# Upper halves of two weight matrices, laid out in 16 blocks whose starts differ by 512 bytes

## The chip, the core and the metric

The kernel runs on one core of one Trainium2 chip. Such a core has five engines that run side by side and wait for each other through semaphores: TensorE (PE, the matmuls; its loads of the stationary operand are shown apart as PEld), VectorE (DVE), ScalarE (ACT), GpSimd (POOL) and SyncE (SP), which starts the DMAs. Operands lie in SBUF, 128 partitions of bytes; matmuls write to PSUM. The metric is the time of one execution on the device in microseconds, the median of several runs.

## The reference

A sliding-window attention (64 keys back, 8 heads of 64) feeds a two-layer block with a softmax-weighted activation and a norm. Cut to what matters:

```python
scores = scale * q @ k^T                    # 8 batches, 8 heads, 576 positions, 64 wide
attn   = softmax(where(0 <= i - j < 64, scores, -1e9))
x      = (attn @ v)                         # 4608 rows x 512
h      = x @ w_in                           # 4608 x 1024
solu   = h * softmax(h)
ln     = (solu - mean) / sqrt(var + 1e-6) * g_ln
out    = ln @ w_out                         # 4608 x 512
```

## The kernel before

The 4608 rows are worked in 36 tiles of 128. For each tile the kernel loads q, k and v, computes the scores on TensorE (line 460), the softmax on DVE, ACT and POOL (lines 475 to 500), transposes it, multiplies by v (line 559), then runs the two matrix products of the block: `moe_in` (line 603, x times w_in into `pH`) and `moe_out` (line 737, the normed rows times w_out into `pO`).

Those two products are made of three matmuls in place of one, to keep float32 accuracy with one pass per matmul: each operand is split into an upper half (rounded to the type that TensorE reads in one pass, float32r) and a lower half (what the rounding left out). A product is then x upper times w upper, x upper times w lower, x lower times w upper. So the names are: `xH`, `xL` and `yH`, `yL` for the rows, `w_inH` and `w_outH` for the upper halves of the weights, and the ring tile `w` for the lower halves (`WL`). In each matmul the rows are the stationary operand (128 x 128, loaded by a LDWEIGHTS of its own) and 512 columns of a weight are the moving operand. A row tile takes 24 matmuls of line 603 and 24 of line 737; in each, 16 move an upper half and 8 a lower half, in the order H, lower, H, lower, H, H. Tiles 0 to 2 (line 590) and 0 to 1 (line 724) use plain float32 matmuls on unsplit weights instead.

The upper halves are written once, by `split` (lines 386 to 400): for each of 16 blocks of 512 columns ACT writes the block through `WH(i, x)` and DVE reads it back to make the lower half. From then on only TensorE reads them. Before the change a block is a slice of `w_inH` [128, 4, 1024] or of `w_outH` [128, 8, 512]. Each block is 2048 bytes of a partition.

Where they lie follows from the order of the declarations. The tiles ahead of them and the unnamed tile `shift` put `w_inH` at byte 20416 of a partition, which leaves 448 when divided by 512. Both weights are 16384 bytes, so each of the 16 blocks begins at remainder 448. `g_sb` (32 bytes), the unnamed tile `gap` (960) and `neghalf` (32 with its rounding up) fill 1024, and all the rings behind (`qk`, `w`, `xH`, `yH`, ...) have sizes that are multiples of 512, so each row operand, each of its 512-byte column groups, and each lower half begins at remainder 448 too. A LDWEIGHTS reads 512 bytes of a partition.

The order of the work is made by the class `Plan`, a list scheduler with fixed costs that looks at operations and tiles, not at addresses. All engines then run their instructions in the planned order.

Of the kernel before, what the change touches and what calls it, by code (L numbers as in the profile page):

```python
# [9 lines left out]
F32 = mybir.dt.float32  # L10
F32R = mybir.dt.float32r
# [8 lines left out]
P = 128  # L20
# [47 lines left out]
SPL = 3  # L68
RATE = 240

PADS = 12
PAD_S = 0
PAD_P = 0
# [153 lines left out]
def tile_window_attention_solu_moe(  # L227
# [19 lines left out]
    NT, DM = out.shape  # L247
    w_in, w_out = w_in.bitcast(I32), w_out.bitcast(I32)
    DFF = w_in.shape[1] // 2
# [3 lines left out]
    NC = DM // P  # L253
    NF = DFF // P
# [4 lines left out]
    const = ctx.enter_context(tc.tile_pool(name="const", bufs=1))  # L259
# [25 lines left out]
            nc.gpsimd.memset(t[first * WIN:(first + 1) * WIN, :WIN], NEG)  # L285

    const.tile([P, 272], F32, name="shift")
    w_inH = const.tile([P, NC, DFF], F32R, name="w_inH")
    w_outH = const.tile([P, NF, DM], F32R, name="w_outH")
    g_sb = const.tile([P, NF], F32, name="g_sb")  # L290
    const.tile([P, 240], F32, name="gap")
    neghalf = const.tile([P, 1], F32, name="neghalf")
    nc.gpsimd.memset(neghalf, -0.5)

# [20 lines left out]
        return T("w", NW + i, [P, 2, 512], F32R)  # L315

    def WH(i, x):
        if i < NC:
            return w_inH[:, i, x * 512:(x + 1) * 512]
        return w_outH[:, 2 * (i - NC) + x]  # L320

    def weight_block(i, src):

# [62 lines left out]
    def split(i):  # L386

        for x in range(2):
            reads = [("w", i), ("w", i, x), ("w", NC + 1 if i < NC else NW - 1)]
            last = reads[:2] + [("H", i, x)], [("w", NW + i, x)]  # L390
            if i < NC:
                plan.op("ACT", 600, lambda x=x: nc.scalar.copy(WH(i, x), W32(i)[:, x]), reads, [("H", i, x)])
                plan.op("DVE", 690, lambda x=x: nc.vector.tensor_sub(
                    WL(i)[:, x], W32(i)[:, x], WH(i, x).bitcast(F32)), *last, port=True)
                continue
            f = 2 * (i - NC) + x
            plan.op("ACT", 600, lambda x=x, f=f: nc.scalar.mul(WH(i, x), W32(i)[:, x], g_sb[:, f:f + 1]),
                    reads + [("g",)], [("H", i, x)])
            plan.op("DVE", 690, lambda x=x, f=f: nc.vector.scalar_tensor_tensor(
                WL(i)[:, x], W32(i)[:, x], g_sb[:, f:f + 1], WH(i, x).bitcast(F32), ALU.mult, ALU.subtract), *last, port=True)  # L400
# [27 lines left out]
    def SS(t):  # L428
        return T("sS", t, [P, H, P])
# [38 lines left out]
    def softmax(t):  # L468
# [16 lines left out]
        def rec():  # L485
            return T("rec", t, [P, H], pool=st)
# [3 lines left out]
        for o in range(0, H, n):  # L490
# [6 lines left out]
            for h in range(o, o + n):  # L497
                plan.op(engine, cost, lambda h=h: v.tensor_scalar(  # L498
                    SS(t)[:, h], SS(t)[:, h], rec()[:, h:h + 1], 0.0, ALU.mult, ALU.add),
                    [R], [("sS", t, h)], PAD_S if t >= PADS else 0, port=True)  # L500

# [3 lines left out]
    def XP(t):  # L505
        return T("raw", NW + 2 * t, [P, 4, 2, 512], U16)

    def cross(t):
        if t < CROSS_P:
            return  # L510
        for x in range(2):
# [4 lines left out]
                XP(t)[:, 2 + x].rearrange("p w (h n) -> p (w h) n", h=4), XP(t)[:, x].rearrange("p w n -> p (w n)")),  # L516
                [("raw", NW + 2 * t, x)], [("raw", NW + 2 * t, 2 + x)], PAD_P if t >= PADS else 0, t > SPL)

# [137 lines left out]
    def EP(t, h):  # L656
        return XB(t)[:, h]

    def TP(t, h):
        return XB(t)[:, 2 + h].rearrange("p w (f n) -> p w f n", f=4)  # L660

    def moe_cross(t):
        if not crosses(t):
            return
        for h in range(2):
# [4 lines left out]
                TP(t, h).rearrange("p w f n -> p (w f) n"), EP(t, h).rearrange("p w n -> p (w n)")),  # L670
                [("raw", NW + 2 * t + 1, h)], [("raw", NW + 2 * t + 1, 2 + h)], PAD_E if t >= PADS else 0, t > SPL)

# [227 lines left out]
```

## Time and profile before

| | |
|---|---|
| runs | 511.93, 512.82, 513.01 us; median 512.82 |
| span of the profiled execution, first to last instruction | 510.9 us |
| around the span (median less span) | 1.9 us |
| busy: PE, PEld, DVE, ACT, POOL | 492.1, 392.4, 409.8, 355.6, 314.5 us |
| matmuls of lines 603 and 737 | 1608, of which 1072 move an upper half |

The profiled execution has no time of its own beside its span; the 1.9 us is the median of the runs less that span. A matmul's duration in the rows includes its way through the array, so two matmuls that follow each other overlap; what a matmul costs is the distance from its start to the next one's start. I call that its spacing. The chain of waits, in order of time, sums up such runs: a piece "5.44 PE pH L603 x24" is 24 spacings.

### The profile page before, as it was taken

What the parts mean: (1) busy time and instruction counts of PE and PEld (TensorE: products, weight loads), DVE (VectorE), ACT (ScalarE), POOL (GpSimd) and SP (SyncE); (2) the same over time, 40 slices, a digit from 0 to 9 for tenths busy, and PEclk for the clock granted to TensorE, in tenths of its full rate; (3) what the DMA queues carried; (4) which work ended last, traced back from release to release, by engine and by line L of the source; (5) the groups of instructions that cost most, each with busy time, mean ns of one, the idle gap of its engine ahead of it and who ended that gap; (6) DMA issues with size and microseconds to landing.
All of it is one profiled execution on the core that took longest, in us unless ns stands there. A gap on an engine that the chain in (4) does not pass through costs nothing.

```text
span 510.9 us, 11601 instructions
## 1 busy us (share of the span) xinstructions
PE 492.1 (96%) x4064; PEld 392.4 (77%) x4064; DVE 409.8 (80%) x1176; ACT 355.6 (70%) x960; POOL 314.5 (62%) x566
## 2 busy tenths in 40 slices
PE   2889999999999999999999999999999999999996
PEld 1445577888788888888888888888888888888885
DVE  5998997888796989787978898887878878977531
ACT  4589795868686777777776868686859586865331
POOL 4388467664757475758574858584848485936430
PEclk9999999999999999999999999999999999999999
DMA  8994446966889989898889797879897969764301
GB/s 321 412 410 177 116 120 119 234 156 147 173 219 148 234 164 229 171 223 163 229 151 243 143 250 145 250 141 247 132 244 144 267 117 222 124 131 103 83 21 43
DMA packets 150762, 94.09 MB, mean 184 GB/s; under 512 B 135088, under 2 KB 135344, under 8 KB 150320
## 3 DMA queue, kind: packets, MB, share of 16 engines
q1 hardware_dynamic: 150704, 93.35, 76.7%
q8 instruction: 32, 0.52, 0.5%
q14 instruction: 26, 0.21, 0.1%
HBM read 50.86 MB, written 9.44 MB: 118 GB/s over the span
## 4 chain that ended last, share of the span: by engine, by line
PE 85%; DVE 4%; ACT 2%; POOL 2%; DMA 2%; issue 0%; SPq 0%; ACTq 0%; DVEq 0%; POOLq 0%
PE pH L603 34%; PE pO L737 34%; PE pO L559 6%; PE pS L460 6%; PE pO L724 3%; PE pH L590 1%; DMA raw<-raw 1%; ACT sS L480 1%; POOL sS L498 1%; PE pS L700 1%; DVE e L623 1%; DVE mst L618 1%; DMA y<-ot 1%; ACT e L620 0%; DVE w L368 0%
## 5 line engine op out<-in xcount | busy, mean ns | idle before, releaser
L498 POOL TENSOR_SCALAR sS<-sS,rec 128x128 f32<-128x128 f32 x280 | 149.2, 554 | 10.8 <-PE pS L460 7.4
L480 ACT ACTIVATE sS<-sS,nmx 128x128 f32<-128x128 f32 x288 | 111.5, 389 | 1.5 <-DVE nmx L475 1.4
L737 PE MATMUL pO<-w_outH,yH 128*128 128x512 f32 x272 | 108.2, 398 | 0.0
L737 PE MATMUL pO<-w,yH 128*128 128x512 f32 x272 | 106.1, 390 | 0.0
L603 PE MATMUL pH<-w_inH,xH 128*128 128x512 f32 x264 | 103.7, 393 | 0.8 <-DVE mst L623 0.8
L603 PE MATMUL pH<-w,xH 128*128 128x512 f32 x264 | 101.8, 389 | 0.0
L737 PE MATMUL pO<-w_outH,yL 128*128 128x512 f32 x272 | 83.9, 389 | 0.0
L512 ACT COPY raw<-sS 128x1024 uint16<-128x1024 uint16 x64 | 66.6, 1046 | 22.9 <-POOL sS L498 22.7
L603 PE MATMUL pH<-w_inH,xL 128*128 128x512 f32 x264 | 81.9, 389 | 0.0
L640 POOL TENSOR_SCALAR e<-e,mst 128x512 f32<-128x512 f32 x72 | 66.8, 936 | 3.9
L632 POOL TENSOR_SCALAR mst<-mst 128x1 f32<-128x1 f32 x36 | 19.9, 553 | 79.8 <-ACT sq L629 42.9
L522 DVE COPY PT<-raw 128x1024 uint16<-128x1024 uint16 x64 | 50.0, 789 | 19.9 <-DMA raw<-raw 19.7
L573 ACT CAST xH<-pO 128x512 fp32r<-128x512 f32 x33 | 19.3, 586 | 63.5 <-PE pO L559 63.4
L737 PEld LDWEIGHTS pO<-w_outH,yH 128*128 128x128 f32 x272 | 51.0, 188 | 12.7 <-issue 2.6
L618 DVE TENSOR_REDUCE mst<-pH 128x1 f32<-128x1024 f32 x36 | 44.0, 1221 | 20.1 <-PE pH L603 20.0
L737 PEld LDWEIGHTS pO<-w_outH,yL 128*128 128x128 f32 x272 | 51.1, 188 | 10.9
L603 PEld LDWEIGHTS pH<-w_inH,xH 128*128 128x128 f32 x264 | 49.6, 188 | 12.2 <-PE pO L737 1.2
L737 PEld LDWEIGHTS pO<-w,yH 128*128 128x128 f32 x272 | 51.1, 188 | 10.0
L603 PEld LDWEIGHTS pH<-w_inH,xL 128*128 128x128 f32 x264 | 49.6, 188 | 10.6 <-issue 0.2
L603 PEld LDWEIGHTS pH<-w,xH 128*128 128x128 f32 x264 | 49.6, 188 | 10.4 <-issue 0.2
L626 POOL TENSOR_SCALAR mst<-mst 128x1 f32<-128x1 f32 x36 | 18.9, 524 | 62.3 <-DVE mst L623 56.5
L629 ACT ACTIVATE sq<-e,mst 128x1024 bf16<-128x1024 f32 x36 | 41.4, 1150 | 21.6 <-POOL mst L626 21.6
(71 smaller groups left out, 852.3 us busy)
## 6 DMA issues: line engine op xcount, KB each, us to landing
qk<-qk SPq DMA_DIRECT2D x36, 640.0 KB, 5.9
v<-vS SPq DMA_DIRECT2D x36, 512.0 KB, 4.7
y<-ot SPq DMA_DIRECT2D x35, 256.0 KB, 2.7
raw<-w_out SPq DMA_DIRECT2D x4, 1024.0 KB, 12.0
raw<-w_in SPq DMA_DIRECT2D x3, 1024.0 KB, 11.5
raw<-raw SPq DMA_TRANSPOSE x126, 3.2
raw<-w_in SPq DMA_DIRECT2D x2, 512.0 KB, 6.2
y<-ot SPq DMA_DIRECT2D x2, 128.0 KB, 1.7
```

The lines of the kernel that those rows point to most:

```text
L460: nc.tensor.matmul(PS(t, p // 2)[half * WIN:(half + 1) * WIN, r, p], q[rs, p, half * WIN:(half + 1) * WIN], keys, start=True, stop=True)
L480: plan.op("ACT", 390, lambda h=h: nc.scalar.activation(SS(t)[:, h], SS(t)[:, h], AF.Exp, bias=cols("nmx", h), scale=-1.0, accum_out=cols(" ...
L498: plan.op(engine, cost, lambda h=h: v.tensor_scalar(SS(t)[:, h], SS(t)[:, h], rec()[:, h:h + 1], 0.0, ALU.mult, ALU.add), [R], [("sS", t, ...
L512: plan.op("ACT", 1050, lambda x=x: nc.scalar.copy(XP(t)[:, x], SS(t)[:, 4 * x:4 * x + 4].bitcast(U16).rearrange("p h (n w) -> p w (h n)", ...
L522: plan.op("DVE", 740, lambda x=x: nc.vector.tensor_copy(PT(t)[:, 4 * x:4 * x + 4].bitcast(U16).rearrange("p h (n w) -> p h w n", w=2), XP( ...
L559: nc.tensor.matmul(PX(t, p)[r * D:(r + 1) * D, p, ks], V(t, half)[:, h * D:(h + 1) * D], PT(t)[:, h, ks], start=True, stop=True)
L603: plan.op("PE", 235, lambda n=n, c=c, d=d, x=x, w=w: nc.tensor.matmul(PH(t)[:, d * 512:(d + 1) * 512], x(t)[:, c], WH(c, d) if w is WH els ...
L618: plan.op("DVE", 1225, lambda: nc.vector.tensor_reduce(nmax(), PH(t), axis=AX.X, op=ALU.max, negate=True), [("pH", t)], [key(0)])
L629: plan.op("ACT", 1150, lambda: nc.scalar.activation(T("sq", t, [P, DFF], BF16), E(t), AF.Square, bias=nmean(), scale=1.0, accum_out=ss()), ...
L632: plan.op("POOL", 240, lambda: nc.gpsimd.tensor_scalar(kk(), ss(), se(), se(), ALU.mult, ALU.mult), [key(1), key(3)], [key(5)])
L640: plan.op("POOL", 770, lambda h=h, hs=hs: nc.gpsimd.tensor_scalar(E(t)[:, hs], E(t)[:, hs], nmean(), kk(), ALU.add, ALU.mult), [key(4), ke ...
L737: plan.op("PE", 235, lambda n=n, f=f, i=i, x=x, y=y, w=w: nc.tensor.matmul(PO(), y(t)[:, f], w(i, x), start=(n == 0), stop=(n == len(passe ...
```

## The change

The two tiles become flat, with 64 columns (256 bytes) more each. Block n begins STEPS[n] bytes behind its old place within its tile. Blocks don't overlap, since the steps rise within each tile. `w_inH` stays at byte 20416; `w_outH` moves up by the 256 bytes that `w_inH` has grown by; `gap` shrinks by the 512 that both have grown by, so all that lies behind it stays where it was.

```diff
+STEPS = [16, 32, 48, 64, 96, 112, 128, 192, 0, 80, 144, 160, 176, 208, 224, 240]
...
     const.tile([P, 272], F32, name="shift")
-    w_inH = const.tile([P, NC, DFF], F32R, name="w_inH")
-    w_outH = const.tile([P, NF, DM], F32R, name="w_outH")
+    WOFF = [512 * n + x // 4 for n, x in enumerate(STEPS)]
+    w_inH = const.tile([P, 8 * 512 + 64], F32R, name="w_inH")
+    w_outH = const.tile([P, 8 * 512 + 64], F32R, name="w_outH")
     g_sb = const.tile([P, NF], F32, name="g_sb")
-    const.tile([P, 240], F32, name="gap")
+    const.tile([P, 112], F32, name="gap")
...
     def WH(i, x):
-        if i < NC:
-            return w_inH[:, i, x * 512:(x + 1) * 512]
-        return w_outH[:, 2 * (i - NC) + x]
+        w, n = (w_inH, 2 * i + x) if i < NC else (w_outH, 8 + 2 * (i - NC) + x)
+        o = WOFF[n] - n // 8 * 4096
+        return w[:, o:o + 512]
```

Counted from the remainder 448 that everything else keeps, the eight blocks of `w_inH` now begin 16, 32, 48, 64, 96, 112, 128 and 192 bytes on. The eight of `w_outH` begin 256, 336, 400, 416, 432, 464, 480 and 496 bytes on, the 256 of the moved tile included. No block keeps the remainder 448. The order of instructions is the same on all five engines, and so are their shapes and the tiles that they wait for.

## Rows read from the trace of the kernel before

**Rows 1.** The page's busy times and the chain that ended last.

```profile
PE 492.1 (96%) x4064; PEld 392.4 (77%) x4064; DVE 409.8 (80%) x1176; ACT 355.6 (70%) x960; POOL 314.5 (62%) x566
...
PE 85%; DVE 4%; ACT 2%; POOL 2%; DMA 2%; issue 0%; SPq 0%; ACTq 0%; DVEq 0%; POOLq 0%
```

**Rows 2.** Busy us by engine in stretches, then granted clock, DMA share, GB/s.

```profile
100.00:200.00 100.00, 99.23 (x902) 82.11 (x901) 83.05 (x242) 71.33 (x188) 62.29 (x114) 1.00 0.87 188
200.00:300.00 100.00, 100.00 (x881) 83.50 (x880) 83.93 (x230) 72.69 (x197) 66.88 (x117) 1.00 0.85 194
300.00:400.00 100.00, 100.00 (x795) 83.15 (x795) 83.45 (x253) 73.74 (x204) 67.46 (x120) 1.00 0.89 187
400.00:460.00 60.00, 60.00 (x550) 50.18 (x547) 51.09 (x157) 44.65 (x123) 39.09 (x66) 1.00 0.80 168
```

**Rows 3.** The chain in order of time: start us, length us, engine, tile, line.

```profile
195.87 5.67 PE pO L737 x24
201.54 5.44 PE pH L603 x24
206.98 5.44 PE pO L737 x24
212.42 5.44 PE pH L603 x24
221.78 5.67 PE pO L737 x24
```

**Rows 4.** PE in order of time, 195.8 to 201.4 us: start, length, instruction.

```profile
195.80 0.50 PE L737 MATMUL pO<-w_outH,yH 128*128 128x512 f32 x1
196.13 0.39 PE L737 MATMUL pO<-w,yH 128*128 128x512 f32 x1
196.36 0.39 PE L737 MATMUL pO<-w_outH,yH 128*128 128x512 f32 x1
196.59 0.40 PE L737 MATMUL pO<-w,yH 128*128 128x512 f32 x1
196.83 0.62 PE L737 MATMUL pO<-w_outH,yL 128*128 128x512 f32 x2
197.29 0.39 PE L737 MATMUL pO<-w_outH,yH 128*128 128x512 f32 x1
197.52 0.39 PE L737 MATMUL pO<-w,yH 128*128 128x512 f32 x1
```

**Rows 5.** PE in order of time from 89.5 us, after another start.

```profile
89.53 0.50 PE L737 MATMUL pO<-w_outH,yH 128*128 128x512 f32 x1
89.87 0.40 PE L737 MATMUL pO<-w,yH 128*128 128x512 f32 x1
90.10 0.40 PE L737 MATMUL pO<-w_outH,yH 128*128 128x512 f32 x1
90.34 0.40 PE L737 MATMUL pO<-w,yH 128*128 128x512 f32 x1
90.57 0.62 PE L737 MATMUL pO<-w_outH,yL 128*128 128x512 f32 x2
91.03 0.40 PE L737 MATMUL pO<-w_outH,yH 128*128 128x512 f32 x1
91.26 0.39 PE L737 MATMUL pO<-w,yH 128*128 128x512 f32 x1
91.49 0.40 PE L737 MATMUL pO<-w_outH,yH 128*128 128x512 f32 x1
91.72 0.39 PE L737 MATMUL pO<-w,yH 128*128 128x512 f32 x1
91.95 0.39 PE L737 MATMUL pO<-w_outH,yL 128*128 128x512 f32 x1
```

**Rows 6.** The stationary loads in order of time, 195.8 to 197.3 us.

```profile
195.79 0.19 PEld L737 LDWEIGHTS pO<-w_outH,yH 128*128 128x128 f32 x1 [0.17 <-issue]
195.90 0.19 PEld L737 LDWEIGHTS pO<-w,yH 128*128 128x128 f32 x1
196.14 0.19 PEld L737 LDWEIGHTS pO<-w_outH,yH 128*128 128x128 f32 x1
196.37 0.19 PEld L737 LDWEIGHTS pO<-w,yH 128*128 128x128 f32 x1
```

**Rows 7.** Plain float32 matmuls of line 724, PE in order of time.

```profile
60.90 3.17 PE L724 MATMUL pO<-w,yH 128*128 128x512 f32 x7
```

**Rows 8.** Same line, all of it: duration ns least/median/most, first and last start.

```profile
L724 PE MATMUL pO<-w,yH x32: 592/592/697, 56.9 to 79.0; 128*128 128x512 f32 x32
```

**Rows 9.** Matmuls that move an upper half: count, busy us, mean ns, idle before.

```profile
L737 PE MATMUL pO<-w_outH,yH 128*128 128x512 f32 x272 | 108.2, 398 | 0.0
L603 PE MATMUL pH<-w_inH,xH 128*128 128x512 f32 x264 | 103.7, 393 | 0.8 <-DVE mst L623 0.8
L737 PE MATMUL pO<-w_outH,yL 128*128 128x512 f32 x272 | 83.9, 389 | 0.0
L603 PE MATMUL pH<-w_inH,xL 128*128 128x512 f32 x264 | 81.9, 389 | 0.0
```

**Rows 10.** The writers and the other reader of the upper halves, same columns.

```profile
L393 DVE TENSOR_TENSOR w<-w,w_inH 128x512 fp32r<-128x512 f32 x8 | 5.9, 772 | 1.2 <-ACT w_inH L392 1.1
L399 DVE SCALAR_TENSOR_TENSOR w<-w,g_sb,w_outH 128x512 fp32r<-128x512 f32 x8 | 5.8, 750 | 0.1
L397 ACT ACTIVATE w_outH<-w,g_sb 128x512 fp32r<-128x512 f32 x8 | 5.1, 716 | 0.0
L392 ACT CAST w_inH<-w 128x512 fp32r<-128x512 f32 x8 | 4.5, 611 | 0.0
```

## The prediction

> **What bounds the kernel now.** I read the page first: PE is busy for 96% of the span and makes up 85% of the chain that ended last [rows 1]. The table of stretches says where: from 200 to 460 us PE is busy without a gap, at a granted clock of 1.00, that is 2.4 GHz, while DVE, the next busiest, stands at 51 to 84 us of 60 to 100 [rows 2]. So in the steady part a nanosecond that a matmul loses or gains is a nanosecond of the time. What matters is then the spacing of the matmuls of lines 603 and 737, start to start, not their durations of 389 to 398 ns [rows 9], which overlap.
>
> The chain in order of time gives the spacing. A block of 24 matmuls in the middle of a run takes 5.44 us, 5.44 / 24 = 226.7 ns each, whether its weights are w_inH or w_outH and whichever ring buffers its rows lie in [rows 3]. The first block after a stop of this stream (the small matmuls of lines 460 and 559 lie between) takes 5.67 us. The list of PE's instructions shows why [rows 4]: the start itself, 195.80 to 196.13, is 0.33 us long, and then the next six matmuls run from 196.13 to 197.52, which is 1390 / 6 = 231.7 ns each, 5 ns over the later pace. In the start at 89.5 us it lasts longer: from 89.87 to 91.95 lie nine spacings, 2080 / 9 = 231.1 ns [rows 5]. Single ones of these differ (196.36 to 196.59 is 0.23, 196.59 to 196.83 is 0.24).
>
> So the pace is no constant of the instruction. It begins at about 231.5 ns and settles, after six to nine matmuls, at 226.7. Kind and size of the matmuls are the same throughout, and nothing waits. What does run beside each matmul is the load of the next one's stationary operand: it starts within 0.01 us of the matmul's start in each pair [rows 4, 6], so two streams read SBUF at once, 2048 bytes a partition for the moving columns and 512 for the load. And 226.7 is not what the columns alone take: 512 columns at 2.4 GHz are 213.3 ns, so 13.3 ns are added. The plain matmuls of line 724 show less: seven records in 3.17 us, the last of them 0.592 long [rows 7, 8], so (3.17 - 0.592) / 6 = 430 ns apart. Those move the same 512 columns twice in a record (427 ns), at half the bytes per unit of time, and only 3 ns are added. I read this as the two streams getting in each other's way when the moving one runs at full rate, by an amount that depends on how they stand to each other, with a settled state at which they lose 13.3 ns a matmul and an unsettled one at which they lose 18. No row shows the collision itself; this is inference from the spacing.
>
> **The change part by part.** It adds and removes no instruction, and the order is the same on each engine, so no wait moves. It touches 16 writes by ACT, 16 reads by DVE and 1072 moving reads by PE.
>
> The writes and reads of `split`: 8 + 8 on ACT at 611 and 716 ns, 8 + 8 on DVE at 772 and 750 [rows 10]. They keep shape and type. Even a tenth of these would be 16 x 0.07 = 1.1 us on each engine, once and early, before the steady part, beside a PE that is busy with lines 590 to 737. I cost them at nothing; without that cover 1.1 us would be their price.
>
> The loads of the stationary operand and the moving reads of the lower halves (536 matmuls) keep their addresses. The 1072 upper-half matmuls [rows 9] keep their count, but the moving read now begins 16 to 496 bytes off the remainder at which the load beside it begins, another amount for each block. In the old kernel each pair of streams had the same distance (zero by 512), matmul after matmul, and on that the pace could settle. In the new one the distance changes with each upper-half matmul, between neighbours too. The likeliest is that it then stays unsettled: 231.5 ns in place of 226.7, the mean of the two starts, 4.8 ns more.
>
> The sum: starts such as those of [rows 4, 5], pieces of 5.67 us or more in the chain like the first and last of [rows 3], stand about 20 times in the trace, so some 20 x 6 = 120 matmuls already run at the unsettled pace, two thirds of them, 80, with an upper half. That leaves 1072 - 80 = about 990. 990 x 4.8 ns = 4.8 us. On the span of 510.9 that is 515.7, and with the 1.9 us between span and median **517.6 us**.
>
> The price per matmul is the unknown, as no row shows a moving read at another distance, so I bound it. Above: 240 ns, the longest single spacing in those rows (196.59 to 196.83, read to 0.01 us), for all 990, 13.3 x 990 = 13.2 us, 526.0. Below: the plain matmul's 3 ns in place of 13.3, so 10.3 x 1072 = 11.0 us less, 501.8. I take 4.8 ns because those rows are the same instruction with the same operands, only not settled.
>
> The Trainium skill (SBUF — State Buffer, section "Who interferes with whom") states that PE has two independent read ports, one for the moving operand and one for LDWEIGHTS, and that PE never waits on anyone. By that the start address would be free, since the steps of 16 bytes also keep its 16-byte lines whole, and the time would be that of the rival "no effect" below. The settling in [rows 4, 5] speaks against it, since two independent streams have nothing to settle. The skill's TensorE: Matmul & The Clock Gate (section "Wait — 56ns, not 53.3ns?") gives 215.7 ns from start to start for 512 columns at full clock; the trace has 226.7, 11 ns more, and the plain matmuls agree with a small fixed cost.
>
> **The rivals.**
>
> *The lower halves are dragged along* (still slower). The settling runs across matmuls, so an unsettled upper half may leave the next lower half unsettled too: about 1490 matmuls at 4.8 ns, 7.2 us, 520.0. For it: in both starts the lower-half spacings are no shorter than their neighbours [rows 4, 5].
>
> *No effect.* The 226.7 may be a fixed cost of this kind of matmul, and the longer spacings after a start may come from the start (a queue that fills, a supply that settles) and not from addresses. Then nothing changes: **512.8 us**. For it: the pace is the same for both weight tiles and all ring buffers; but these have all the same remainder, so it says little.
>
> *The distance sets the streams free* (not slower). If the loss of 13.3 ns comes from both streams beginning at the same remainder, so that they ask for the same part of SBUF in step, any distance could remove it, wholly or at some of the 16 blocks. All blocks: 501.8 as above; half of the blocks, the others unchanged: 512.8 - 5.5 = **507.3**. It decides at a mean spacing below 226.7. For it: the plain matmuls lose only 3 ns. Against it: the unsettled pace, at which the streams stand otherwise to each other, is longer and not shorter in both starts.
>
> *The change doesn't do what it says.* The remainders follow from sizes; only the base of w_outH could surprise, and its 256 bytes are counted. I give this nothing of its own.
>
> If the matmuls got faster by the full 11 us, what comes next is no wait: DVE has 16 us of each 100 free [rows 2], so most of a gain would arrive.
>
> **How the numbers follow.** Slower by one of the two unsettled cases: 0.54 (0.36 for upper halves alone at 517.6, 0.18 for more, around 520). No effect, within 0.2% (512.82 +- 1.0, about what a measurement of this kernel can tell from no change): 0.25. Faster: 0.21, of which half below 508. The forecast is the likeliest single case, 517.6. The range: from 508 (leaving out about 0.11 below) to 522 (leaving out about 0.09 of the cases near the upper bound).
>
> **What the new profile would show.** If I am right, middle blocks of the chain take 5.44 + 16 x 0.0048 = 5.52 us or, with the lower halves, 5.56, instead of 5.44; the mean durations of the four upper-half groups rise from 389 by some 5 ns; the pace differs from block to block of the weights; DVE, ACT and POOL keep their busy times. If all middle blocks still take 5.44, address has no effect. If they take 5.3 or less, the free-streams rival holds, and the spacing by block tells at which distances. Wrong altogether would be a change in waits or in the granted clock.

## The result and the profile after

The changed kernel takes 518.63 us (518.42 to 518.75, median of 4 runs) against 512.51 us for the kernel before, the median of four runs, three of which stand in the table above. The medians differ by 6.1 us. The ratio of the runs is given as 1.0115, with a 95% interval of 1.0097 to 1.0133 (the two medians alone give 1.0119), so the changed kernel is slower. The span of the profiled execution is 516.5 us, 5.6 more than before.

The page of the changed kernel, the lines that answer to [rows 1]: busy time by engine, and the chain that ended last.

```profile
PE 497.3 (96%) x4064; PEld 392.3 (76%) x4064; DVE 408.0 (79%) x1176; ACT 355.8 (69%) x960; POOL 314.4 (61%) x566
...
PE 91%; DVE 1%; ACT 1%; issue 0%; ACTq 0%
```

PE is 5.2 us longer busy, and it has become more of the chain (91% for 85%). The other engines do what they did, within 2 us. The granted clock stays at full, as the stretches of the changed kernel show, which answer to [rows 2] (columns as there):

```profile
100.00:200.00 100.00, 100.00 (x901) 82.12 (x901) 82.49 (x242) 71.55 (x189) 62.98 (x113) 1.00 0.85 185
200.00:300.00 100.00, 100.00 (x823) 82.05 (x825) 81.35 (x230) 71.77 (x197) 67.42 (x118) 1.00 0.85 189
```

Where the time came from stands in the chain in order of time, which answers to [rows 3] (lines 605 and 739 are the old 603 and 737):

```profile
170.30 5.76 PE pO L739 x24
176.06 5.55 PE pH L605 x24
181.61 5.54 PE pO L739 x24
187.15 5.55 PE pH L605 x24
...
196.62 5.76 PE pO L739 x24
```

Every block of 24 matmuls is longer: 5.55 for 5.44 in line 605, 5.54 for 5.44 in the middle of line 739, 5.76 for 5.67 after a stop. The same in the mean durations of the matmuls that move an upper half, which answer to [rows 9]:

```profile
L739 PE MATMUL pO<-w_outH,yH 128*128 128x512 f32 x272 | 109.3, 402 | 0.0
L605 PE MATMUL pH<-w_inH,xH 128*128 128x512 f32 x264 | 105.0, 398 | 0.0
L739 PE MATMUL pO<-w_outH,yL 128*128 128x512 f32 x272 | 84.7, 393 | 0.0
L605 PE MATMUL pH<-w_inH,xL 128*128 128x512 f32 x264 | 83.1, 393 | 0.0
```

Each is 4 to 5 ns over its row before. The sum closes roughly: the trace has 33 blocks of line 605 at 0.11 us more (3.6), 17 middle blocks of line 739 at 0.10 (1.7) and 17 after a stop at 0.09 (1.5), together 6.8 us. About 1.2 of it is covered by two waits of the kernel before that are gone now. From 133.00 and from 185.84 us of its trace two spacings each are long, 1157 and 310 ns, 379 and 307 ns, where 227 is usual. PE of the kernel before, in order of time:

```profile
132.78 0.61 PE L737 MATMUL pO<-w_outH,yL 128*128 128x512 f32 x2
134.16 0.47 PE L603 MATMUL pH<-w_inH,xH 128*128 128x512 f32 x1 [0.77 <-DVE mst L623]
134.47 0.39 PE L603 MATMUL pH<-w,xH 128*128 128x512 f32 x1
...
185.62 0.61 PE L737 MATMUL pO<-w_outH,yL 128*128 128x512 f32 x2
186.22 0.47 PE L603 MATMUL pH<-w_inH,xH 128*128 128x512 f32 x1
186.53 0.39 PE L603 MATMUL pH<-w,xH 128*128 128x512 f32 x1
```

The idle time of 0.77 us between 100 and 200 us in [rows 2] is a part of this. The rest, 5.6, stands beside 5.6 of the span and 6.1 of the medians.

The start of every matmul in the trace gives the spacings apart by what is moved (spacings over 290 ns, at stops and waits, left out): upper halves 231.6 ns for 227.0 before, lower halves 230.8 for 227.3. So the lower halves, whose addresses and loads didn't change, became slower too. A spacing ends at the start of the next matmul, so how the loss is shared between two neighbours follows from this way of counting.

### The profile page after: what moved, and what is told of

Its sections match the earlier page's. It is cut to its first block, busy times and chain, and to the rows that moved or that the text cites. A ratio compares the mean times of both kernels' runs of the same rounds, so it can differ in the third digit from the quotient of the medians.

```text
span 516.5 us, 11601 instructions
## 1 busy us (share of the span) xinstructions
PE 497.3 (96%) x4064; PEld 392.3 (76%) x4064; DVE 408.0 (79%) x1176; ACT 355.8 (69%) x960; POOL 314.4 (61%) x566
## 4 chain that ended last, share of the span: by engine, by line
PE 91%; DVE 1%; ACT 1%; issue 0%; ACTq 0%
PE pO L739 37%; PE pH L605 35%; PE pO L561 7%; PE pS L462 6%; PE pO L726 3%; PE pH L592 3%; PE pS L702 1%; DVE sS L477 0%; DVE yL L713 0%; DVE w L367 0%; ACT e L622 0%; ACT yH L711 0%; DVE mst L620 0%; DVE e L625 0%; PE pS L535 0%
## 5 line engine op out<-in xcount | busy, mean ns | idle before, releaser
L739 PE MATMUL pO<-w_outH,yH 128*128 128x512 f32 x272 | 109.3, 402 | 0.0
L605 PE MATMUL pH<-w_inH,xH 128*128 128x512 f32 x264 | 105.0, 398 | 0.0
L605 PE MATMUL pH<-w_inH,xL 128*128 128x512 f32 x264 | 83.1, 393 | 0.0
L634 POOL TENSOR_SCALAR mst<-mst 128x1 f32<-128x1 f32 x36 | 19.4, 540 | 79.4 <-ACT sq L631 42.7
L628 POOL TENSOR_SCALAR mst<-mst 128x1 f32<-128x1 f32 x36 | 17.2, 477 | 68.8 <-DVE mst L625 62.6
```

Source lines behind the costliest of these rows:

```text
L605: plan.op("PE", 235, lambda n=n, c=c, d=d, x=x, w=w: nc.tensor.matmul(PH(t)[:, d * 512:(d + 1) * 512], x(t)[:, c], WH(c, d) if w is WH els ...
L634: plan.op("POOL", 240, lambda: nc.gpsimd.tensor_scalar(kk(), ss(), se(), se(), ALU.mult, ALU.mult), [key(1), key(3)], [key(5)])
L739: plan.op("PE", 235, lambda n=n, f=f, i=i, x=x, y=y, w=w: nc.tensor.matmul(PO(), y(t)[:, f], w(i, x), start=(n == 0), stop=(n == len(passe ...
```

## The experiments

In what follows the distance is that by which the row operand (the stationary one) begins on from the weights (the moving one), or the other way round where the text says so.

**One distance for a whole run, 16 to 256 bytes.** All weights keep their old remainder. The row operands get 512 bytes more room, and begin `DIST` bytes on, another amount for each run of matmuls between two stops.

```diff
+DIST = [0, 16, 32, 48, 64, 80, 96, 112, 128, 144, 160, 176, 192, 208, 224, 240, 256, 0]
+    def rows(tag, t, dtype, c, run):
+        o = DIST[max(run, 0)] // 4
+        return T(tag, t, [P, c * P + P], dtype)[:, o:o + c * P].rearrange("p (c n) -> p c n", c=c)
     def XH(t):
-        return T("xH", t, [P, NC, P], F32 if t < PLAIN_IN else F32R)
+        return rows("xH", t, F32 if t < PLAIN_IN else F32R, NC, (t - 3) // 2)
```

(`xL`, `yH` and `yL` likewise, the last two with `t // 2`.)

> All weights stay where they were before the change (remainder 448). Only the row operands xH, xL, yH, yL move: all 96 matmuls of one run between two stops read their stationary operand at one distance from the moving one, 16 bytes in the first run, 32 in the next, up to 256 in the last. Theory (the distance between the two streams sets the pace): the settled pace differs between runs, 226.7 ns is near the least of them, most lie between 227 and 236, so blocks of 24 take 5.44 to 5.66 us, and the time is 513 to 520 us. Rival (only the remainder at which the moving read begins counts): no moving address changes, all middle blocks take 5.44 us, time 512.5.

Measured: 520.17 us, ratio 1.0146 (1.0125 to 1.0166), 0.2 over the expected range. The chain of this kernel in order of time (lines 608 and 742 are 603 and 737), one middle block from the runs at 64, 96, 176, 192, 240 and 256 bytes:

```profile
177.17 5.60 PE pH L608 x24
...
230.10 5.62 PE pH L608 x24
...
362.58 5.52 PE pH L608 x24
...
388.77 5.49 PE pH L608 x24
...
466.90 5.48 PE pH L608 x24
...
490.11 5.45 PE pH L608 x24
```

No moving read begins at another remainder than before, and yet the blocks differ from run to run and are alike within one. The rival on the moving remainder alone falls.

**The same, 272 to 496 bytes.** The same edit with another table; the last run is at 0.

```diff
+DIST = [0, 272, 288, 304, 320, 336, 352, 368, 384, 400, 416, 432, 448, 464, 480, 496, 0, 0]
```

> As the scan with distances 16 to 256, with 272 to 496 bytes and a last run at 0. Theory: paces of 227 to 236 ns that differ from run to run, and 226.7 in the last run at 0; 513 to 520 us. Rival (moving remainder alone): 5.44 us for every middle block, 512.5.

Measured: 519.89 us, ratio 1.0140 (1.0120 to 1.0160). The chain in order of time, the runs at 320, 352, 432, 448, 496 and 0 bytes:

```profile
176.66 5.60 PE pH L608 x24
...
229.59 5.62 PE pH L608 x24
...
362.08 5.52 PE pH L608 x24
...
388.27 5.49 PE pH L608 x24
...
466.39 5.48 PE pH L608 x24
...
489.61 5.45 PE pH L608 x24
```

Line by line the same as the first scan: a distance and the same plus 256 give the same block. So the period is 256 bytes, not 512. Over one period, from the middle blocks of both:

| row operands begin on by (bytes) | block of 24, us | ns each |
|---|---|---|
| 0 | 5.44 | 226.7 |
| 240 | 5.48 | 228.3 |
| 192 | 5.49 | 228.8 |
| 176 | 5.52 | 230.0 |
| 80, 128, 208 | 5.57 | 232.1 |
| 16, 32, 48, 64, 112, 144, 160, 224 | 5.60 | 233.3 |
| 96 | 5.62 | 234.2 |

Zero is the best of the 16. The mean of the 16 is (5.44 + 5.48 + 5.49 + 5.52 + 3 x 5.57 + 8 x 5.60 + 5.62) / 16 = 5.57 us, 231.9 ns.

**All of it 32 bytes on.**

```diff
-    const.tile([P, 272], F32, name="shift")
+    const.tile([P, 280], F32, name="shift")
```

> All of it, weights and row operands, begins at remainder 480 instead of 448, so each pair of streams keeps its distance of zero. Theory (distance): the settled pace stays 226.7 ns and the time 512.5 us. Rival (the remainder of the moving read itself, 448 being a good one): a pace of about 231 ns, some 6 us more, 518.

Measured: 512.67 us, ratio 0.9998 (0.9986 to 1.0009); middle blocks 5.44. A shift of 32 bytes that all operands share does nothing.

**The flat layout with whole steps of 512.**

```diff
-STEPS = [16, 32, 48, 64, 96, 112, 128, 192, 0, 80, 144, 160, 176, 208, 224, 240]
+STEPS = [0, 512, 1024, 1024, 1536, 2048, 2048, 2048, 0, 0, 512, 512, 1024, 1024, 1536, 2048]
```

(with 512 columns more in each tile, and `gap` as it was.)

> The flat layout of the change, but each block is moved by 0, 512, 1024, 1536 or 2048 bytes, so it keeps its remainder. Theory and the rival on the moving remainder: 512.5 us, blocks of 5.44 us. Rival (it is the layout or the place as such, other blocks of SBUF, and not the remainder by 512): up to the 518.6 of the change.

Measured: 512.75 us, ratio 0.9997 (0.9986 to 1.0008). Neither the flat tile nor the place of the blocks is the cause.

**Upper halves alone, all 32 bytes on.** `shift` as above, and `gap` 8 columns smaller, so that the rest stays.

```diff
-    const.tile([P, 240], F32, name="gap")
+    const.tile([P, 232], F32, name="gap")
```

> The 16 upper-half blocks all begin 32 bytes on (remainder 480), in their old layout; lower halves and row operands stay at 448. So each run alternates between distance 32 and distance 0, as H, lower, H, lower, H, H. In the scan, where all matmuls of a run had the same distance, 32 settled at 233.3 ns and 0 at 226.7. Theory without memory (each matmul pays for its own distance): upper halves 233.3, lower halves 226.7, sum 1072 x 6.6 = 7.1 us, 520. Rival (the lower halves are dragged along): lower halves at 230 ns or more, 521 to 523. Older theory (what counts is that the distance changes from one matmul to the next): about 231.5 for both, 520.

Measured: 521.55 us, ratio 1.0173 (1.0147 to 1.0199), the slowest of all. PE in order of time in a settled run of this kernel:

```profile
204.35 0.40 PE L603 MATMUL pH<-w_inH,xH 128*128 128x512 f32 x1
204.58 0.40 PE L603 MATMUL pH<-w,xH 128*128 128x512 f32 x1
204.82 0.39 PE L603 MATMUL pH<-w_inH,xH 128*128 128x512 f32 x1
205.05 0.39 PE L603 MATMUL pH<-w,xH 128*128 128x512 f32 x1
205.28 0.63 PE L603 MATMUL pH<-w_inH,xL 128*128 128x512 f32 x2
205.75 0.40 PE L603 MATMUL pH<-w_inH,xH 128*128 128x512 f32 x1
```

Six spacings in 1.40 us, 233.3 each, and the pattern repeats every six. That is the scan's pace at this distance (weights 32 on are rows 224 on, by 256), but here for all six, although two of them stand at distance 0. The longest is not an upper half but the first lower half, from 204.58 to 204.82; by the starts of the whole trace the lower halves average 234.4 and the upper halves 232.3. A price for each matmul by its own distance would have left the lower halves at 226.7 and the time at 520. That theory falls, and the rival holds: the lower halves are dragged along.

**The steps for w_in alone.**

```diff
-STEPS = [16, 32, 48, 64, 96, 112, 128, 192, 0, 80, 144, 160, 176, 208, 224, 240]
+STEPS = [16, 32, 48, 64, 96, 112, 128, 192, 0, 0, 0, 0, 0, 0, 0, 0]
```

(`w_inH` has 128 columns more than before the change and `w_outH` none, so that w_out and all behind it keep their remainder.)

> The steps of the change for the eight blocks of w_in alone; w_out keeps remainder 448 throughout. Theory (a price for each distance, paid where it stands): about half of the 6 us of the change, 515 to 516, with line 603's blocks of 24 at 5.55 us and line 737's at 5.44 but for six or so unsettled matmuls at each change between the two lines, so up to 5.50. Rival (any disturbance keeps the whole run unsettled): both lines at 5.55, 518.

Measured: 515.68 us, ratio 1.0057 (1.0039 to 1.0075), half of the change. The chain in order of time:

```profile
169.45 5.66 PE pO L739 x24
175.11 5.55 PE pH L605 x24
180.67 5.46 PE pO L739 x24
186.12 5.55 PE pH L605 x24
```

Line 739, at distance 0 again, is back at 5.46 within one block. So the drag is short: it reaches the neighbours, not the whole run.

**Finer than 16 bytes.** The scan with other distances.

```diff
+DIST = [0, 4, 8, 12, 20, 24, 28, 252, 248, 244, 236, 232, 228, 132, 136, 140, 0, 0]
```

> As the first two scans, but the row operands lie 4, 8, 12, 20, 24, 28 and 252, 248, 244, 236, 232, 228 bytes on, one distance to a run, then 132, 136, 140. Theory (the distance counts, and whole 16-byte steps are only a grid on it): paces that lie between those of the neighbours on the grid, 226.7 to 234; if one is below 226.7, a uniform layout at that distance beats both kernels. Rival (only whole 16-byte lines count): 4, 8, 12 behave as 0 or as 16, that is 226.7, 228.3 or 233.3, nothing between.

Measured: 519.27 us, a single run. The chain in order of time, the runs at 4, 8, 12, 20, 252 and 132 bytes:

```profile
108.35 5.57 PE pH L608 x24
...
123.58 5.53 PE pH L608 x24
...
149.84 5.52 PE pH L608 x24
...
176.10 5.60 PE pH L608 x24
...
255.45 5.60 PE pH L608 x24
...
413.81 5.44 PE pH L608 x24
```

Four bytes either way are enough to leave the good pace: 4 on gives 232, 4 back 233.3. The pace is not smooth in the distance either, since 132 bytes give 5.44 and its neighbours 128 and 136 give 5.57 and 5.60. Both expectations missed in part: there are values between those of the grid, but they don't lie in order. None is under 226.7, so no uniform distance tried beats the kernel before. How a pace settles shows best at 12 bytes, PE in order of time:

```profile
149.68 0.39 PE L608 MATMUL pH<-w_inH,xH 128*128 128x512 f32 x1
149.90 0.40 PE L608 MATMUL pH<-w,xH 128*128 128x512 f32 x1
150.14 0.39 PE L608 MATMUL pH<-w_inH,xH 128*128 128x512 f32 x1
150.36 0.40 PE L608 MATMUL pH<-w,xH 128*128 128x512 f32 x1
150.60 0.62 PE L608 MATMUL pH<-w_inH,xL 128*128 128x512 f32 x2
```

The spacings are 0.22, 0.24, 0.22, 0.24: short and long in turn, for all of the run, between matmuls of the same distance. So within this run the distance holds the mean pace, but what a single matmul takes depends also on what ran before it.

**Upper halves alone, 256 bytes on.** `shift` 336 columns, `gap` 176.

> The 16 upper-half blocks all begin 256 bytes on (remainder 192); all else stays at 448. The scans gave the same pace for each distance d and d + 256. Theory (the distance counts by 256, not by 512): 512.5 to 513 us, middle blocks 5.44. Rival (by 512, or the moved weights differ from moved rows): up to 518.

Measured: 512.71 us, ratio 1.0002 (0.9987 to 1.0017), middle blocks 5.44. Moved weights and moved rows agree: it is the distance, by 256.

**Another order, and half loads.** Two kernels with the six matmuls of each pair in another order; in the first `M` gives 128 throughout, and the second loads and uses only 64 stationary columns for the lower rows. The lines of `moe_in` (line 737 likewise):

```diff
-... for d, k in ((0, 0), (0, 1), (1, 0), (1, 1), (0, 2), (1, 2))]
+... for d, k in ((0, 0), (0, 2), (1, 0), (1, 2), (0, 1), (1, 1))]
-                PH(t)[:, d * 512:(d + 1) * 512], x(t)[:, c], ...
+                PH(t)[:M(x is XL), d * 512:(d + 1) * 512], x(t)[:, c, :M(x is XL)], ...
+    def M(low):
+        return 64 if low else P
```

> The six matmuls of each pair of column blocks come in another order: H by upper rows, H by lower rows, twice, then the two lower halves. All distances stay zero. Theory (distance zero settles whatever the order): 226.7 ns, blocks of 5.44 us, 512.5 to 513.5 us. It is the comparison for the half load.

Measured: 512.62 us, ratio 0.9999 (0.9988 to 1.0010), blocks of 5.44.

> The same order, but the matmuls by xL and yL load and use only the first 64 of 128 stationary columns, so two of six loads read 256 bytes a partition instead of 512; this leaves out the product of lower rows and upper weights for the second 64 rows of each tile. The moving read is unchanged. Theory (what a matmul loses is lost to the load that runs beside it): the two matmuls of six that run beside a half load come down towards 220 ns (half of the 13.3 lost), blocks of 24 from 5.44 to 5.39 us or less, 508 to 510 us. Rival (the 13.3 ns belong to the moving read alone): 226.7 throughout, 5.44, time as the reordered kernel.

Measured: 516.64 us, two runs, ratio 1.0083 (1.0054 to 1.0112). With shorter loads the kernel is slower. The loads in order of time, and the chain in order of time of this kernel:

```profile
197.41 0.13 PEld L740 LDWEIGHTS pO<-w_outH,yL 128*64 128x64 f32 x1
197.63 0.19 PEld L740 LDWEIGHTS pO<-w_outH,yH 128*128 128x128 f32 x1
197.87 0.14 PEld L740 LDWEIGHTS pO<-w_outH,yL 128*64 128x64 f32 x1
```

```profile
175.50 5.52 PE pH L606 x24
181.02 5.52 PE pO L740 x24
```

The loads are shorter, 0.13 for 0.19 us, and the distance is zero everywhere, but the blocks rose from 5.44 to 5.52, 230 ns each. So both expectations fall: the 13.3 ns are not a loss in proportion to what the load reads, and the pace did not stay as it was, though the moving read is the same. That it is the load which changes the pace is not shown: a matmul with 64 stationary columns also writes 64 partitions of PSUM in place of 128, and no run tells the two apart.

**The steps in rising order.**

```diff
+STEPS = [0, 16, 32, 48, 64, 80, 96, 112, 128, 144, 160, 176, 192, 208, 224, 240]
```

> The change with its 16 steps in rising order, so the blocks of w_in begin 0 to 112 bytes on and those of w_out 384 to 496: by 256 the same 16 distances, given to other blocks. Theory (each distance has its price, and the spread pays about their mean, 232 ns, on the matmuls that it reaches): 518 to 519 us again. Rival (the sequence of distances decides, not their set): outside 517 to 520, up to 522 or down to 515.

Measured: 519.42 us, ratio 1.0121 (1.0090 to 1.0152), with middle blocks of 5.58 and 5.56. The same set of distances in another sequence costs about the same, 0.02 to 0.03 us a block more than the change. The time is 0.4 over the 518 to 519 expected and within the 517 to 520 outside which the rival was to hold.

## Why the prediction came out

**What bounds the kernel: right.** PE's spacing set the time, and what it lost arrived, but for the 1.2 us that the two earlier waits covered.

**That the address counts: right.** Against "no effect", the scans changed nothing but where the stationary operand lies, and the middle blocks went from 5.44 to as much as 5.62. The Trainium skill's rule (SBUF — State Buffer, section "Who interferes with whom"), that PE's two read ports are independent and PE never waits on anyone, is at odds with these runs for this pair of streams. The rival of streams set free falls as well: no distance of the three scans gave a pace under 226.7.

**The price of an upper half, 4.8 ns: right in size.** The starts give 231.6 for 227.0, 4.6 ns, where the prediction had 231.5 for 226.7. The reason given for it fails, as said below, so that the unsettled matmuls after a start were a fair sample is luck as far as the runs show. The scans offer another sum: the change takes 16 distances that by 256 are all multiples of 16, one each, and the mean of their paces is 231.9. But the blocks of the changed kernel don't pay these prices one by one, though their paces differ as predicted, from 228.0 to 237.1 ns. By the starts in the last three blocks of 24 of each run of 96 matmuls, the upper halves of the block at distance 0 by 256 take 232.4 ns (226.7 in the scan), those of the block whose distance is the dearest of the scan (rows 96 on, 234.2) take 229.9, and the dearest block, 237.1, stands at a distance (rows 160 on) that the scan has at 233.3. So that the mean comes out does not show that each block pays for its own distance.

**The lower halves at nothing: wrong.** This is the term that was mis-sized. The forecast of 517.6 left 536 lower halves at their old pace, and gave the case in which they are dragged along 520.0. The trace has 230.8 for 227.3, 3.5 ns over 535 spacings, 1.9 us. Upper halves at 4.6 over 1072 are 4.9 us; with both, 6.8, as in the sum over the blocks, and the 1.2 that earlier waits cover brings it to the 5.6 of the span. So the time lies between the two cases. In the kernel with all upper halves 32 bytes on the drag is larger still, 234.4 ns for the lower halves.

**The reason, that the distance changes from matmul to matmul and the pace therefore stays unsettled: wrong as it stands.** In the scans nothing changes within a run, and the pace does settle; but it settles dearer, at 228 to 234 ns, on patterns that repeat every few matmuls. So a distance that stays the same costs too. A reader who had followed that step would have expected each run at one uniform distance to settle at 226.7; of the 16 distances in the first two scans only zero does. And all upper halves at one distance, 32 bytes on, cost 9.0 us (521.55 against 512.59), more than the spread with its 6.1. Whether the change from matmul to matmul adds a cost of its own, no run tells.

**By 512: wrong, by 256.** It made no difference here, since one block (of w_out, 256 bytes on) alone stands at a distance that by 256 is zero, and it is dragged with its neighbours (the 232.4 ns above).

**What stays open.** The prediction read the 13.3 ns over pure streaming as the load's share. The half loads speak against a loss in proportion to the load, and nothing was tried that takes the load away. Shown are two things: the pace depends on the distance between stationary and moving operand, and a single spacing depends on what ran before. That the length of the load counts is not shown, since its run changes what PE writes as well. How the two reads meet inside the chip is not shown, nor what a mixture of distances costs block by block.

## What to carry to other kernels

Where one-pass float32 matmuls bound a kernel (here with 128 x 128 stationary and 512 moving columns, each with a load of its own; no other shape was run), put stationary and moving operand at starts that are equal by 256 bytes, for every pair; that was 226.7 ns a matmul here, and other distances cost up to 234, even for neighbours that keep a good distance. Look at the spacing of starts in time order, not at mean durations alone. A spacing that takes a few matmuls to settle after a stop, among matmuls of one kind that wait for nothing, is worth following up: here such a dependence stood behind it. That its unsettled values came near what the spread of addresses costs holds for this one case and is not a rule.

## What had not been expected of the hardware

- The dependence repeats by 256 bytes, and 4 bytes are enough to leave the best pace (226.7 to 232 and 233.3 ns).
- At a fixed distance the spacing may settle on a cycle, at 12 bytes 0.22 and 0.24 us in turn.
- Two of six matmuls with 64 stationary columns in place of 128 and the same moving read made the stream slower (230 for 226.7 ns), not faster.
- With mixed distances the blocks don't keep the paces of the scan: the block at distance 0 took 232.4 ns, the one at the dearest distance 229.9.
- A distance of 132 bytes gave 226.7 as well, while 128 and 136 gave 232 and 233.3.
